# Taps and w1 loaded in halves between pairs of x loads, and logits over interleaved channels

## The chip, the cores and the metric

One core of one Trainium2 chip runs the kernel. The metric is the device time of one execution in microseconds. Before the change, three runs took 309.0, 310.02 and 312.22 us; the median is 310.02 us. A later run is compared with runs of the kernel before on the same chip.

## The reference

All of it is float32. First a causal convolution with weights that differ by position and head, then a soft mixture of experts over all 28672 rows:

```python
w = softmax(weight_gen)                       # [8, 3584, 8 heads, 7 taps], over the taps
x_unf = windows of 7 rows of x                # x: [8, 3584, 192], 8 heads x 24 channels
y = einsum('bshk,bskhg->bshg', w, x_unf)      # -> [28672, 192]
logits = y @ phi                              # phi: [192, 32 slots], 8 experts x 4
d = softmax(logits, axis=0)                   # over the 28672 rows
slot_input = d.T @ y                          # [32, 192]
slot_out[e] = relu(slot_input[e] @ w1[e]) @ w2[e]    # w1: [192, 1024], w2: [1024, 192]
out = softmax(logits, axis=1) @ slot_out      # [28672, 192]
```

## The kernel before

**Blocks and pairs.** The rows are cut into blocks of 26 positions; four of them are a *group* (276 groups), two groups a *pair* (138), four groups a *supergroup* (69, the unit of an x load), four pairs a *block k* (35), eight pairs a *unit u* (17, and a last one of two pairs). So two supergroups make a block k and four a unit.

**Loads.** `loadx(t)` (line 153) is four DMAs, one for each h, of 32 partitions and 96 KB together per DMA; they fill one of five places of `big`, block-diagonally over the four heads of a half. A place is free again when the convolution of the supergroup five earlier has read it. `loadw(c)` (line 158) is one DMA that brings the taps of a *chunk c* into one of three buffers; chunk c serves block k = c. The two parts of the expert weights w1 come as 24 DMAs of 128 partitions and 512 columns (line 571). All are issued on SP in the order of the list `ops`, one after the other; each waits for what it overwrites, and those behind it wait with it.

**The chain of a chunk** (`chain`, line 472): the largest tap (`tap_top`, DVE), the subtraction (`tap_sub`, POOL), the exponential (`tap_exp`, ACT), the sum in three additions (`tap_sum`, POOL), its reciprocal (`tap_inv`, DVE), the product (`tap_mul`, POOL, into `wide`), and a 32x32 transposition (`tap_turn`, DVE) that makes the band matrices (`band`) of one block k.

**TensorE, by block k:** `conv` of the four pairs (16 products of 96 columns each, into a PSUM buffer `cv`; ACT copies it to `tm`), and `xpose`, twelve transpositions whose results ACT copies to `cm`, with channels on partitions. Each odd block also holds, behind its third pair, `dispatch` (line 337), the sum of d.T @ y for the unit before; each even block holds, behind its second pair, `logits` (line 274), 16 products of 208 columns into `ls`. DVE takes the largest logit (`top`, line 285: names mx and mq), TensorE spreads it (`newmax`, line 304), DVE reduces it (`newmax_out`, line 308: nm), ACT takes the exponentials (`dexp`), and DVE transposes them (`dturn`: dt). On even groups the two halves of the heads lie in one order in `cv`, on odd groups in the other, so that three tiles of 128 channels hold a pair; four pieces of phi (`phi_sb`) fit them.

**The order.** Each piece of work is an entry of `ops`: engine, cost, what it reads and writes, and `late`, how much later than the end of its cost its result is there (for a load, the landing). TensorE and SP keep the order of the list. For DVE, ACT and POOL, `model` (line 616) plays the list through with these costs and landings and takes, at each step, the ready entry whose latest allowed time is the earliest. The order found is fixed in the program. An engine does its entries in that order whatever the real times are.

**After the convolution** the last unit is finished, the constants `selO4` (over phi's tile) and `si` are written by POOL (lines 689 and 690), the slot inputs go through the experts (lines 703 to 806), and the output phase (line 832) multiplies, copies and stores 22 MB.

Of the kernel before, what the change touches and what calls it, by code (L numbers as in the profile page):

```python
# [10 lines left out]
ALU = mybir.AluOpType  # L11
# [25 lines left out]
Q = 4  # L37
# [8 lines left out]
def place(t):  # L46
    return t % NXS if t else NXS - 1
# [3 lines left out]
def conv_soft_moe(ctx, tc, xh, wh, phi, w1a, w1b, w2, out):  # L51
# [100 lines left out]
    mq = keep.tile([128, 5], F32, name="mq")  # L152
    def loadx(t):

        for h in range(4):
            SY.dma_start(xbd[32 * h : 32 * h + 32, place(t), h], xh[t, h])

    def loadw(c):
        n = min(CH, NG // 4 - CH * c)
        SY.dma_start(taps[c % NTAP][:, 0:n], wh[c, :, 0:n])  # L160

    ALL = slice(0, CH)
    tops, tsums = {}, {}

# [56 lines left out]
    def conv(p):  # L221
        cv = cvs[p % NCV]
        for par in range(2):
            g = 2 * p + par
            t = g // SGG
            for c in range(2):
                for blk in range(4):
                    o = 4 * GW * (2 * par + (c ^ par))
                    i, b = ((4 * (g % m) + blk) * 2 + c for m in (4, SGG))
                    P.matmul(cv[32 * blk : 32 * blk + T, o : o + 4 * GW],  # L230
                             bands[g // 8 % NBAND][:, g // 4 % CH, :, i],
                             xbd[:, place(t), :, b * GW : (b + 1) * GW], start=True, stop=True)
# [41 lines left out]
    def logits(u, lo=0, hi=UP):  # L274
        hi = min(hi, UNITS[u][1])
        cm = cms[u]
        lp = lss(u).rearrange("p (a b) j -> p a b j", b=2)
        for par in range(2):
            for i in range(2):
                for blk in range(4):  # L280
                    P.matmul(lp[32 * blk : 32 * blk + 32, lo:hi, par, 0:T],  # L281
                             phi_sb[:, 2 * par + i, :], cm[:, lo:hi, 1 if i else 2 * par, blk, :],
                             start=(i == 0), stop=(i == 1))

# [132 lines left out]
    def pace(e, what, src):  # L417
        op(PO, 0.15, [what], [("w2", e), x_of(NSG - NXS + e // 2)], mark, e, src)
        op(SP, 0.4, [("w2", e)], [], loadw2, e)
# [22 lines left out]
    def x_of(t):  # L442
        return ("x", place(t))

    def conv_reads(p):
        return {x_of(g // SGG) for g in (2 * p, 2 * p + 1)} | {("band", p // 4 % NBAND, p // 2 % CH)}

# [6 lines left out]
    op(SP, 0.65, [], [("w", 1, 0), ("w", 1, 1)], loadw, 1, late=2.6)  # L454
    op(SP, 2.6, [], [x_of(0)], loadx, 0, late=2.8)
    op(SP, 0.6, [], [("w", 2, 0), ("w", 2, 1)], loadw, 2, late=3.0)
    op(SP, 1.9, [], [x_of(1)], loadx, 1, late=3.0)
    for t, es in ((2, (PO, AC, AC, AC)), (3, (PO, AC, VE, AC)), (NXS, (PO, PO, AC, AC))):
        for h, e in enumerate(es):
            op(e, 0.77, [], [("z", t, h)], clear, place(t), h, {PO: G, AC: A, VE: V}[e])  # L460
        if t < NXS:
            op(SP, 1.9, [("z", t, h) for h in range(4)], [x_of(t)], loadx, t, late=3.0)
    for i in range(NCV):
# [81 lines left out]
    for k in range(BLOCKS):  # L545
# [8 lines left out]
        for c in range(3, NCH):  # L554
            if k == max(0, c - 2):
                chain(c)
        for c in range(NTAP, NCH):
            if k == max(0, c - 4):
                op(SP, 0.4, [], [("w", c % NTAP, b) for b in range(CH)], loadw, c, late=4.0)
        for t in range(NSG):  # L560
            if (SGG * t + SGG - 1) // (2 * Q) == k:
                if t + NXS < NSG:
                    for i in (NXS - 1, NXS) if t == 0 else (t + NXS,):
                        op(SP, 2.0, [("z", i, h) for h in range(4)], [x_of(i)], loadx, i, late=3.0)
                    if t == 0:
                        op(SP, 0.45, [], ["phi"], SY.dma_start, phi_sb, phi, late=3.0)
                for j in range(2 * (E + E // 2)):
                    if 2 + 5 * j // 2 == t:
                        e, f = j // 2, slice(F // 2 * (j % 2), F // 2 * (j % 2 + 1))
                        to, w, e = (w1a_sb, w1a, e) if e < E else (w1b_sb, w1b, e - E)  # L570
                        op(SP, 0.4, [], [], SY.dma_start, to[:, e, f], w[:, e, f])
        for p in ps:
# [22 lines left out]
    op(TE, 0.19 * n, cm_of(final), [("ls", 1), spare], logits, final)  # L595
    op(VE, 0.4, [], [("ls", 1), "mq"], top, final)
# [91 lines left out]
    bctx = ExitStack()  # L688
    G.tensor_tensor(out=selO4, in0=sel4, in1=selE4, op=ALU.subtract)
    G.memset(si, 0.0)  # L690
    actx.close()
# [12 lines left out]
    P.matmul(pst, accS[:, 1:129], sE, start=True, stop=False)  # L704
    P.matmul(pst[0:96], accS[:, 96:192], sO, start=False, stop=True)
    P.matmul(pst[96:128], accS[:, 0:32], sO, start=False, stop=True)
    V.tensor_copy(siM.rearrange("p (e m) -> p e m", m=DG)[:, :, 0:SE],
# [4 lines left out]
    for r in (0, 64):  # L712
        P.matmul(psu[r : r + 64], accS[:, 129 : D + 1], sE, start=True, stop=False)
        P.matmul(psu[r : r + 64], accS[:, 32:96], sO, start=False, stop=True)
    for u in range(2):
# [168 lines left out]
def _layout(x, weight_gen, moe_phi, moe_w1, moe_w2):  # L884
    import numpy as np

    starts = np.minimum(T * np.arange(NB), S - T)

    xp = np.concatenate([np.zeros((B, KT - 1, D), x.dtype), x], axis=1)
    rows = starts[:, None] + np.arange(L)[None, :]  # L890
    xg = xp[:, rows, :].reshape(NSG, SGG * 4, L, 2, 4, GW)
    xh = xg.transpose(0, 4, 2, 1, 3, 5).reshape(NSG, 4, L, NBC * GW)
# [9 lines left out]
    ph[0] = moe_phi[0:128]
    ph[1, 0:64] = moe_phi[128:192]
    ph[2, 0:32] = moe_phi[160:192]
    ph[2, 32:128] = moe_phi[0:96]
    ph[3, 64:128] = moe_phi[96:160]
    ph = ph.transpose(1, 0, 2)
    w1a = moe_w1[:, 0:128, :].transpose(1, 0, 2)
    w1b = moe_w1[:, 128:D, :].reshape(2, 4, 64, F).transpose(0, 2, 1, 3).reshape(128, 4, F)
    w2 = moe_w2.reshape(E, F // 128, 128, D).transpose(2, 0, 1, 3)  # L910
    return [np.ascontiguousarray(a) for a in (xh, wh, ph, w1a, w1b, w2)]
# [20 lines left out]
```

## Time and profile before

| | before |
|---|---|
| time, median of three runs | 310.02 us (309.0 to 312.22) |
| the profiled execution: time, span | 308.94 us, 307.2 us |
| mean granted TensorE clock | 0.945 |
| busy: PE, DVE, ACT, POOL | 265.4, 197.8, 190.3, 146.5 us |
| SP: issues of x, of taps, of w1 | 276, 35, 24 |
| read from and written to HBM | 46.21 MB, 22.04 MB |

The times of the table are those of one execution; its span runs from the first to the last instruction, and 1.7 us of its time lie around the span. The views used below are: the chain of waits (the work that ended last, in order of time: start, length, what), the windows (busy time of each engine in a stretch, the granted clock and the DMA share), the groups of instructions (by line, engine and operation, with the mean of one), the waits, and the timeline. On SP, a row of the timeline joins neighbouring issues of one kind, and its length runs from the first issue to the end of the last.

### The profile page before, as it was taken

To read this page: it belongs to the slowest core of one execution; us is meant where nothing else is said; L and a number is where in the kernel's file an instruction comes from. 1 tells how busy PE (TensorE), PEld (TensorE's weight loads), DVE (VectorE), ACT (ScalarE), POOL (GpSimd) and SP (SyncE) were. 2 spreads that over 40 slices of the span, in tenths; PEclk is the share of its full clock that TensorE was granted. 3 is DMA by queue.
4 is the path that set the end of the run, shared out by engine and by line. 5 is a ranking of instruction groups with operands and counts; after the bars stand their busy time and mean duration, and the time that the engine had idled before them with its cause. 6 is when DMAs were issued, how large, how long until landed. Compare 5 with 4: busy or idle time off the path is not lost.

```text
span 307.2 us, 15262 instructions
## 1 busy us (share of the span) xinstructions
PE 265.4 (86%) x6646; PEld 213.6 (70%) x6646; DVE 197.8 (64%) x337; ACT 190.3 (62%) x399; POOL 146.5 (48%) x254
## 2 busy tenths in 40 slices
PE   8898996999998999899899989999999888899100
PEld 8887975889887988789788878898768622233000
DVE  8867738775975957868478568573158489994100
ACT  9886673767685778667566666675422188786300
POOL 8856456654568194774654553520027345540000
PEclk9999998999999999999999999999999999879555
DMA  6758666867675767767567667657647079999994
GB/s 184 217 171 236 201 199 195 208 178 207 197 211 150 225 188 207 207 192 212 168 183 212 189 185 211 189 156 227 217 121 296 2 303 403 399 398 398 399 399 177
DMA packets 30161, 69.24 MB, mean 225 GB/s; under 512 B 6288, under 2 KB 11152, under 8 KB 30096
## 3 DMA queue, kind: packets, MB, share of 16 engines
q1 hardware_dynamic: 30096, 68.28, 69.2%
q8 instruction: 52, 0.85, 1.1%
q14 instruction: 13, 0.11, 0.1%
HBM read 46.21 MB, written 22.04 MB: 222 GB/s over the span
## 4 chain that ended last, share of the span: by engine, by line
PE 73%; DVE 6%; DMA 6%; issue 5%; ACT 2%; POOL 2%; DVEq 0%; POOLq 0%; ACTq 0%
PE cv L230 31%; PE pt L250 15%; PE ls L281 8%; PE acb L346 8%; PE po L818 5%; DMA out<-big 4%; PE so L763 2%; PE hpb L742 2%; PE acb L306 2%; DMA taps<-wh 2%; DVE big L825 1%; ACT big L825 1%; DVE band L206 1%; DVE big L362 1%; DVE cT L404 1%
## 5 line engine op out<-in xcount | busy, mean ns | idle before, releaser
L230 PE MATMUL cv<-big,band 128*26 128x96 f32 x4416 | 112.0, 250 | 4.0 <-issue 2.6
L230 PEld LDWEIGHTS cv<-big,band 128*26 128x26 f32 x4416 | 100.8, 130 | 13.8 <-issue 8.1
L236 ACT COPY tm<-cv 128x384 f32<-128x384 f32 x138 | 66.5, 484 | 62.8 <-PE cv L230 62.5
L206 DVE STREAM_TRANSPOSE band<-wide 128x1664 f32<-128x1664 f32 (+1 forms) x37 | 65.4, 1771 | 6.1 <-POOL wide L202 6.0
L250 PE MATMUL pt<-ident,tm 122*128 122x122 f32 x414 | 51.0, 273 | 0.0
L257 ACT COPY cm<-pt 128x416 f32<-128x416 f32 x103 | 48.1, 512 | 1.7 <-PE pt L250 0.6
L250 PEld LDWEIGHTS pt<-ident,tm 122*128 122x128 f32 x414 | 44.7, 145 | 2.3
L202 POOL TENSOR_TENSOR wide<-exps,sum 128x364 f32<-128x364 f32 (+1 forms) x36 | 28.4, 791 | 24.9 <-DVE sum L194 18.6
L818 PE MATMUL po<-cT,so 32*128 32x442 f32 (+3 forms) x256 | 35.4, 644 | 5.6 <-DVE big L825 3.0
L175 POOL TENSOR_TENSOR taps<-taps,top 128x364 f32<-128x364 f32 (+1 forms) x36 | 28.5, 793 | 18.3 <-DVE top L171 17.9
L825 ACT COPY big<-po 128x884 f32<-128x884 f32 (+2 forms) x33 | 28.5, 894 | 9.3 <-PE po L818 5.3
L188 POOL TENSOR_TENSOR si<-exps 128x208 f32<-128x208 f32 x32 | 20.2, 632 | 28.4 <-ACT exps L179 28.0
L818 PEld LDWEIGHTS po<-cT,so 32*128 32x128 f32 (+1 forms) x256 | 12.3, 172 | 27.5 <-ACT big L825 15.7
L281 PE MATMUL ls<-cm,phi_sb 128*32 128x208 f32 x544 | 29.1, 338 | 2.0 <-issue 1.9
L346 PE MATMUL acb<-tm,dt 128*32 128x193 f32 x544 | 27.4, 328 | 3.3 <-issue 3.3
L288 DVE TENSOR_REDUCE mx<-ls 128x1 f32<-128x416 f32 x17 | 10.0, 588 | 28.1 <-PE ls L281 28.1
L87 POOL TENSOR_TENSOR LT<-LT,rm 128x544 f32<-128x544 f32 (+1 forms) x16 | 17.9, 1119 | 17.0 <-DVE rm L85 17.0
L171 DVE TENSOR_REDUCE top<-taps 128x52 f32<-128x364 f32 (+1 forms) x37 | 17.7, 484 | 12.8 <-DMA taps<-wh 12.0
L281 PEld LDWEIGHTS ls<-cm,phi_sb 128*32 128x32 f32 x544 | 17.8, 109 | 7.9 <-issue 3.6
L346 PEld LDWEIGHTS acb<-tm,dt 128*32 128x32 f32 x544 | 17.8, 110 | 7.4 <-issue 4.7
L99 POOL TENSOR_TENSOR LT<-LT,sm 128x544 f32<-128x544 f32 (+1 forms) x16 | 17.9, 1120 | 6.3 <-DVE sm L97 6.2
L825 DVE COPY big<-po 128x884 f32<-128x884 f32 (+2 forms) x16 | 16.7, 1047 | 6.2 <-ACT big L825 2.2
(113 smaller groups left out, 262.3 us busy)
## 6 DMA issues: line engine op xcount, KB each, us to landing
big<-xh SPq DMA_DIRECT2D x276, 96.0 KB, 3.2
out<-big SPq DMA_DIRECT2D x36, 442.0 KB, 6.9
taps<-wh SPq DMA_DIRECT2D x34, 182.0 KB, 3.7
big<-w SPq DMA_DIRECT2D x8, 768.0 KB, 4.5
out<-big SPq DMA_DIRECT2D x11, 468.0 KB, 4.7
w1a_sb<-w1a SPq DMA_DIRECT2D x16, 256.0 KB, 4.2
w1b_sb<-w1b SPq DMA_DIRECT2D x8, 256.0 KB, 3.6
out<-big SPq DMA_DIRECT2D x2, 234.0 KB, 2.3
```

The costliest lines, as they stand in the source:

```text
L175: eng.tensor_tensor(out=t, in0=t, in1=each(tops.pop((c, b.start)), b.stop - b.start), op=ALU.subtract)
L188: eng.tensor_tensor(out=s, in0=t[:, :, :, 0:4], in1=t[:, :, :, 4:8], op=ALU.add)
L202: eng.tensor_tensor(out=dst, in0=exps[c % NEX][:, b, :, 0:KT], in1=each(m, n), op=ALU.mult)
L206: V.transpose(bands[c % NBAND][:, b].rearrange("p b j l -> p (b j l)"), wide[:, b].rearrange("p b j -> p (b j)"))
L230: P.matmul(cv[32 * blk : 32 * blk + T, o : o + 4 * GW], bands[g // 8 % NBAND][:, g // 4 % CH, :, i], xbd[:, place(t), :, b * GW : (b + 1) ...
L236: copy(tms[u % NTM][:, pr, 1 : 2 * D + 1], cvs[p % NCV][:, 0 : 2 * D])
L250: P.transpose(pt[:, at, 0:TR], tms[u % NTM][0:TR, pr, 1 + 128 * i : 129 + 128 * i], ident[0:TR, 0:TR])
L257: copy(cms[u].rearrange("p a i b j -> p (a i b) j")[:, at : at + n], pts.pop((k, j)).rearrange("p i (b j) -> p (i b) j", j=32)[:, 0:n, 0:T])
L281: P.matmul(lp[32 * blk : 32 * blk + 32, lo:hi, par, 0:T], phi_sb[:, 2 * par + i, :], cm[:, lo:hi, 1 if i else 2 * par, blk, :], start=(i = ...
L346: P.matmul(ac[32 * q : 32 * q + 32], dt[:, g, :], tm[:, g // 2, o : o + D + 1], start=(g < 4), stop=(g + 4 >= 2 * n))
L818: P.matmul(po[dst : dst + hi - lo, at, 0 : n * T], so[32 * q : 32 * q + 32, lo:hi], cT[32 * q : 32 * q + 32, g0 : g0 + n, 0:T], start=True ...
L825: (V.tensor_copy if done[1] % 3 == 1 else A.copy)(ot.rearrange("p (q c) -> p q c", c=n * T), po[:, 0 : len(qs), 0 : n * T])
```

## The change

1. **Halves between pairs.** `loadx` issues two of its four DMAs at a time; `loadw` can load 64 of the 128 partitions; w1 comes in 48 DMAs of 64 partitions. In the list, the two halves of a chunk of taps stand each behind the first pair of x DMAs of a supergroup, where the whole chunk stood ahead of the two supergroups. From the fourth chunk on, taps are two DMAs where they were one.
2. **Landings in the list.** `late` of x goes from 3.0 to 3.8 and the cost of four x DMAs from 2.0 to 2.3; `late` of the taps goes from 4.0 to 5.2.
3. **One product of 416 columns.** The products of `conv` now write the 96 columns of a half of the heads interleaved, at a step of eight columns, so that the first 64 or 128 channels of a group are the same channels in every tile; on odd groups the host turns the channels of x by eight. The first and the third tile of a pair then take the same piece of phi, and one product of 416 columns over both replaces two of 208. The host orders the rows of phi and w1 alike.
4. **Constants earlier.** `selO4` and the zeroing of `si` become entries of the list; in the product that uses `selO4`, two products (96 and 32 rows) become one.

```diff
-    def loadx(t):
-        for h in range(4):
+    def loadx(t, hs=range(4)):
+        for h in hs:
             SY.dma_start(xbd[32 * h : 32 * h + 32, place(t), h], xh[t, h])
-    def loadw(c):
+    def loadw(c, r=slice(0, 128)):
         n = min(CH, NG // 4 - CH * c)
-        SY.dma_start(taps[c % NTAP][:, 0:n], wh[c, :, 0:n])
+        SY.dma_start(taps[c % NTAP][r, 0:n], wh[c, r, 0:n])
+    def loadw1(j):
+        e, f, r = j // 4, slice(F // 2 * (j // 2 % 2), F // 2 * (j // 2 % 2 + 1)), HALF[j % 2]
+        to, w, e = (w1a_sb, w1a, e) if e < E else (w1b_sb, w1b, e - E)
+        SY.dma_start(to[r, e, f], w[r, e, f])
...
             for c in range(2):
+                to = cv[:, D * par : D * par + D].rearrange("p (g e) -> p e g", e=H)[:, 4 * c : 4 * c + 4]
                 for blk in range(4):
-                    o = 4 * GW * (2 * par + (c ^ par))
-                    P.matmul(cv[32 * blk : 32 * blk + T, o : o + 4 * GW],
+                    P.matmul(to[32 * blk : 32 * blk + T],
...
+        for blk in range(4):
+            P.matmul(lp[32 * blk : 32 * blk + 32, lo:hi, :, 0:T], phi_sb[:, 0, :],
+                     cm[:, lo:hi, 0:3:2, blk, :], start=True, stop=False)
         for par in range(2):
-            for i in range(2):
-                for blk in range(4):
-                    P.matmul(lp[32 * blk : 32 * blk + 32, lo:hi, par, 0:T],
-                             phi_sb[:, 2 * par + i, :], cm[:, lo:hi, 1 if i else 2 * par, blk, :],
-                             start=(i == 0), stop=(i == 1))
+            for blk in range(4):
+                P.matmul(lp[32 * blk : 32 * blk + 32, lo:hi, par, 0:T], phi_sb[:, 1 + par, :],
+                         cm[:, lo:hi, 1, blk, :], start=False, stop=(par == 1))
...
-        for c in range(NTAP, NCH):
-            if k == max(0, c - 4):
-                op(SP, 0.4, [], [("w", c % NTAP, b) for b in range(CH)], loadw, c, late=4.0)
-        for t in range(NSG):
...
-                        op(SP, 2.0, [("z", i, h) for h in range(4)], [x_of(i)], loadx, i, late=3.0)
...
+        cs = [c for c in range(NTAP, NCH) if k == max(0, c - 4)]
+        parts = [(c, i) for c in cs for i in range(2)]
+        for t in (2 * k, 2 * k + 1):
+            for i in (NXS - 1, NXS) if t == 0 else (t + NXS,) if t + NXS < NSG else ():
+                for j in range(2):
+                    op(SP, 1.15, [("z", i, h) for h in (2 * j, 2 * j + 1)], [x_of(i)[j]],
+                       loadx, i, (2 * j, 2 * j + 1), late=3.8)
+                    if j == 0 and parts and t:
+                        c, h = parts.pop(0)
+                        op(SP, 0.4, [], [("w", c % NTAP, h)], loadw, c, HALF[h], late=5.2)
...
+                for j in range(48):
+                    if 2 + 5 * j // 4 == t:
+                        op(SP, 0.42, [], [], loadw1, j)
+        for c, h in parts:
+            op(SP, 0.4, [], [("w", c % NTAP, h)], loadw, c, HALF[h], late=5.2)
...
+    op(PO, 0.45, ["fold"], ["si"], lambda: G.memset(si, 0.0))
+    op(TE, 0.19 * n, cm_of(final), [("ls", 1), spare, "phi"], logits, final)
+    op(PO, 0.5, ["sel4"], ["phi"], lambda: G.tensor_tensor(out=selO4, in0=sel4, in1=selE4, op=ALU.subtract))
...
-    G.tensor_tensor(out=selO4, in0=sel4, in1=selE4, op=ALU.subtract)
-    G.memset(si, 0.0)
...
-    P.matmul(pst[0:96], accS[:, 96:192], sO, start=False, stop=True)
-    P.matmul(pst[96:128], accS[:, 0:32], sO, start=False, stop=True)
+    P.matmul(pst, accS[:, 64:D], sO, start=False, stop=True)
```

Three places show how instructions move. The first is SP at the start of the program, behind the x of the first supergroup; taps_84, taps_85 and taps_86 are the three buffers of taps, and the first taps row is chunk 2. Before:

```order
L160 DMA taps_86<-wh 128x364
L156 DMA big<-xh 32x768 x12
L160 DMA taps_84<-wh 128x364
L160 DMA taps_85<-wh 128x364
L156 DMA big<-xh 32x768 x8
L686 DMA phi_sb<-phi 128x128
```

After:

```order
L160 DMA taps_86<-wh 128x364
L156 DMA big<-xh 32x768 x20
L698 DMA phi_sb<-phi 128x128
L156 DMA big<-xh 32x768 x2
L160 DMA taps_84<-wh 64x364
L156 DMA big<-xh 32x768 x2
L160 DMA taps_84<-wh 64x364
L160 DMA taps_85<-wh 64x364 x2
L156 DMA big<-xh 32x768 x2
L160 DMA taps_86<-wh 64x364
L156 DMA big<-xh 32x768 x2
L165 DMA w1a_sb<-w1a 64x512
```

Chunks 3 and 4 stood behind 12 x DMAs and now stand behind 22 and 24 of them and phi.

The second place is DVE around the first unit's logits. In the names, the number behind top and sum is the chunk, the number behind mx, nm and dt the unit, and band2 and band0 are the buffers of chunks 2 and 3. Before:

```order
L171 TENSOR_REDUCE top3_0_387<-taps0_84 128x52
L171 TENSOR_REDUCE top4_0_390<-taps1_85 128x52
L206 STREAM_TRANSPOSE band2_92<-wide_89 128x1664
L194 RECIPROCAL sum3_0_453<-sum3_0_453 128x52
L288 TENSOR_REDUCE mx0_525<-ls_99 128x1
L290 TENSOR_SCALAR mq_131<-ls_99,mx0_525 128x4
L206 STREAM_TRANSPOSE band0_90<-wide_89 128x1664
L310 TENSOR_REDUCE nm0_577<-acb_100 128x1
```

After:

```order
L212 STREAM_TRANSPOSE band2_92<-wide_89 128x1664
L295 TENSOR_REDUCE mx0_506<-ls_99 128x1
L297 TENSOR_SCALAR mq_131<-ls_99,mx0_506 128x4
L317 TENSOR_REDUCE nm0_538<-acb_100 128x1
L177 TENSOR_REDUCE top3_0_554<-taps0_84 128x52
L334 STREAM_TRANSPOSE dt0_559<-dd_95 128x512
L177 TENSOR_REDUCE top4_0_563<-taps1_85 128x52
L301 STREAM_TRANSPOSE LT_65<-ls_99 128x512
L200 RECIPROCAL sum3_0_570<-sum3_0_570 128x52
L212 STREAM_TRANSPOSE band0_90<-wide_89 128x1664
```

The first step of chunk 3 stood ahead of chunk 2's band and now stands behind the reduction nm0. On TensorE the order of the blocks is the same in both.

The third place is DVE around the logits of unit 2, with the same names (band1 is the buffer of chunk 7). Before:

```order
L354 SCALAR_TENSOR_TENSOR accS_66<-accS_66,al1_949,acb_100 128x193
L194 RECIPROCAL sum7_0_951<-sum7_0_951 128x52
L171 TENSOR_REDUCE top9_0_998<-taps0_84 128x52
L206 STREAM_TRANSPOSE band1_91<-wide_89 128x1664
L288 TENSOR_REDUCE mx2_1064<-ls_99 128x1
```

After:

```order
L361 SCALAR_TENSOR_TENSOR accS_66<-accS_66,al1_919,acb_100 128x193
L177 TENSOR_REDUCE top8_0_992<-taps2_86 128x52
L200 RECIPROCAL sum7_0_957<-sum7_0_957 128x52
L212 STREAM_TRANSPOSE band1_91<-wide_89 128x1664
L295 TENSOR_REDUCE mx2_1077<-ls_99 128x1
```

The chunk whose taps DVE waits for ahead of mx2 is the eighth where it was the ninth.

More of the change, by code (lines that the diff above doesn't have):

```diff
@@ L417, in pace @@
     def pace(e, what, src):
-        op(PO, 0.15, [what], [("w2", e), x_of(NSG - NXS + e // 2)], mark, e, src)
+        op(PO, 0.15, [what], [("w2", e), *x_of(NSG - NXS + e // 2)], mark, e, src)
         op(SP, 0.4, [("w2", e)], [], loadw2, e)
@@ L442, in x_of @@
     def x_of(t):
-        return ("x", place(t))
+        return [("x", place(t), i) for i in range(2)]
     def conv_reads(p):
-        return {x_of(g // SGG) for g in (2 * p, 2 * p + 1)} | {("band", p // 4 % NBAND, p // 2 % CH)}
+        return {x for g in (2 * p, 2 * p + 1) for x in x_of(g // SGG)} | {("band", p // 4 % NBAND, p // 2 % CH)}
     def tm_of(p):
@@ L461, in conv_soft_moe @@
         if t < NXS:
-            op(SP, 1.9, [("z", t, h) for h in range(4)], [x_of(t)], loadx, t, late=3.0)
+            op(SP, 1.9, [("z", t, h) for h in range(4)], x_of(t), loadx, t, late=3.0)
     for i in range(NCV):
@@ L556, in conv_soft_moe @@
                 chain(c)
-        for c in range(NTAP, NCH):
-            if k == max(0, c - 4):
-                op(SP, 0.4, [], [("w", c % NTAP, b) for b in range(CH)], loadw, c, late=4.0)
-        for t in range(NSG):
-            if (SGG * t + SGG - 1) // (2 * Q) == k:
-                if t + NXS < NSG:
-                    for i in (NXS - 1, NXS) if t == 0 else (t + NXS,):
-                        op(SP, 2.0, [("z", i, h) for h in range(4)], [x_of(i)], loadx, i, late=3.0)
[L565 to L571, printed above, removed]
+        cs = [c for c in range(NTAP, NCH) if k == max(0, c - 4)]
[8 more added lines that the diff above has]
+                        op(SP, 0.4, [], [("w", c % NTAP, h)], loadw, c, HALF[h], late=5.2)
+            if t == 0:
+                op(SP, 0.45, [], ["phi"], SY.dma_start, phi_sb, phi, late=3.0)
+            if 2 <= t < NSG:
+                for j in range(48):
[3 more added lines that the diff above has]
+            op(SP, 0.4, [], [("w", c % NTAP, h)], loadw, c, HALF[h], late=5.2)
         for p in ps:
@@ L713, in conv_soft_moe @@
         P.matmul(psu[r : r + 64], accS[:, 129 : D + 1], sE, start=True, stop=False)
-        P.matmul(psu[r : r + 64], accS[:, 32:96], sO, start=False, stop=True)
+        P.matmul(psu[r : r + 64], accS[:, 0:64], sO, start=False, stop=True)
     for u in range(2):
@@ L899, in _layout @@
     wh = wt.transpose(0, 5, 2, 4, 1, 3, 6).reshape(NCH, 128, CH, T, KT)
+    chan = np.arange(D).reshape(H, GW).T.reshape(D)
+    lo, hi = chan[0:128], chan[128:D]
     ph = np.zeros((4, 128, NS), moe_phi.dtype)
[L902 to L906, printed above, removed]
+    ph[0] = moe_phi[lo]
+    ph[1, 0:64] = moe_phi[hi]
+    ph[2, 64:128] = moe_phi[hi]
     ph = ph.transpose(1, 0, 2)
-    w1a = moe_w1[:, 0:128, :].transpose(1, 0, 2)
-    w1b = moe_w1[:, 128:D, :].reshape(2, 4, 64, F).transpose(0, 2, 1, 3).reshape(128, 4, F)
+    w1a = moe_w1[:, lo, :].transpose(1, 0, 2)
+    w1b = moe_w1[:, hi, :].reshape(2, 4, 64, F).transpose(0, 2, 1, 3).reshape(128, 4, F)
     w2 = moe_w2.reshape(E, F // 128, 128, D).transpose(2, 0, 1, 3)
```

8 lines of the change are left out of this document (5 added, 3 removed).

## The prediction

> **What bounds the kernel now.** I read the windows first: length, then busy time and count of PE, PEld, DVE, ACT and POOL, the granted clock, the DMA share and GB/s.
>
> ```profile
> 24.07:201.07 177.00, 167.14 (x4849) 147.30 (x4852) 123.86 (x197) 117.56 (x266) 101.55 (x177) 0.99 0.68 197
> 102.67:114.38 11.71, 11.71 (x351) 10.33 (x354) 8.32 (x17) 8.61 (x21) 7.18 (x11) 1.00 0.71 204
> 46.00:56.00 10.00, 7.23 (x191) 6.63 (x190) 8.22 (x13) 4.03 (x10) 5.40 (x11) 0.83 0.72 196
> ```
>
> The first stretch is most of the convolution, the second one unit of it in which PE is never idle (351 matmuls; the first has 4849, which is fourteen units of 346). A unit costs 177.00 / 14 = 12.64 us, and 11.71 where nothing waits: 13.1 us are lost. TensorE is the bound and DMA (0.68) is not. The third stretch holds the largest loss: PE idle, and 10.00 x (1 - 0.83) = 1.7 us of clock.
>
> ```profile
> span 307.2 us, 15262 instructions
> DMA  6758666867675767767567667657647079999994
> ```
>
> A slice is 7.68 us. From the 34th slice on, 253.4 us, the DMA engines are full with stores, and before it stand the experts, which need the whole convolution. So a microsecond gained or lost on TensorE before that moves the end by a microsecond.
>
> Next the chain of waits about the third stretch, and the row of PE's waits (total, times, longest):
>
> ```profile
> 42.38 4.68 DMA taps<-wh
> ...
> 47.61 1.82 DVE band L206
> 49.43 0.49 DVE mx L288
> ...
> 50.31 0.36 PE acb L306 x2
> ```
>
> ```profile
> PE acb L306 <- DVE mq L290: 3.2, 2, 2.8
> ```
>
> The taps of chunk 9 are issued at 42.38 and take 4.68 us; DVE stands before them, and behind on DVE stand a band and mx of unit 2, for whose spread PE waits 2.8 us. With the clock, 4.5 us of the 13.1 are here. The other 8.6 are small and spread.
>
> **The change part by part.**
>
> *The wait at mx2.* In the third piece of the order, DVE stands ahead of mx2 before the first step of chunk 8, no longer chunk 9; chunk 8's loads are a block older. The wait goes, and its clock: -4.5. What is late next is the band of chunk 7, which stood there before too.
>
> *Chunk 3's chain.* It now begins behind nm0, and its end is what PE's block 3 needs. PE's rows at that place:
>
> ```profile
> 22.45 0.32 PE acb L306 x2
> 22.77 1.31 PE pt L250 x12
> 24.07 2.14 PE cv L230 x96
> ```
>
> Block 3 starts at 24.07 with no wait. In the changed order DVE can do nm0 from 22.8 and top3 after it, then the chain runs through four engines; the groups (count, busy, mean ns of one, idle before):
>
> ```profile
> L171 DVE TENSOR_REDUCE top<-taps 128x52 f32<-128x364 f32 (+1 forms) x37 | 17.7, 484 | 12.8 <-DMA taps<-wh 12.0 <-POOL taps L175 0.7
> L175 POOL TENSOR_TENSOR taps<-taps,top 128x364 f32<-128x364 f32 (+1 forms) x36 | 28.5, 793 | 18.3 <-DVE top L171 17.9
> L318 ACT ACTIVATE dd<-ls,nm 128x416 f32<-128x416 f32 x17 | 10.5, 616 | 2.4 <-DVE nm L310 1.6
> L257 ACT COPY cm<-pt 128x416 f32<-128x416 f32 x103 | 48.1, 512 | 1.7 <-PE pt L250 0.6
> L179 ACT ACTIVATE exps<-taps 128x364 f32<-128x364 f32 (+1 forms) x37 | 17.9, 493 | 3.9 <-POOL taps L175 3.9
> L188 POOL TENSOR_TENSOR si<-exps 128x208 f32<-128x208 f32 x32 | 20.2, 632 | 28.4 <-ACT exps L179 28.0
> L189 POOL TENSOR_TENSOR si<-si 128x104 f32<-128x104 f32 x32 | 11.6, 362 | 2.5
> L190 POOL TENSOR_TENSOR sum<-si 128x52 f32<-128x52 f32 x32 | 9.2, 288 | 2.5
> L194 DVE RECIPROCAL sum<-sum 128x52 f32<-128x52 f32 (+1 forms) x37 | 16.3, 441 | 2.6 <-POOL sum L190 2.4
> L202 POOL TENSOR_TENSOR wide<-exps,sum 128x364 f32<-128x364 f32 (+1 forms) x36 | 28.4, 791 | 24.9 <-DVE sum L194 18.6 <-ACT tm L236 5.0 <-DMA big<-xh 1.2
> L206 DVE STREAM_TRANSPOSE band<-wide 128x1664 f32<-128x1664 f32 (+1 forms) x37 | 65.4, 1771 | 6.1 <-POOL wide L202 6.0
> ```
>
> Newmax ends at 22.77; I put the end of nm0, a small reduction, at 22.9. From there: top 0.48, subtraction 0.79, exponential 0.49, sum 0.63 + 0.36 + 0.29, reciprocal 0.44, product 0.79, turn 1.77 make 6.04 us, so the band is there at 28.9 and PE waits 4.9 us: the lower bound, with every engine free. ACT is not free: in its new order, the exponentials of unit 0 (0.62, from 23.0) and three copies (0.51 each) stand ahead of chunk 3's exponential, which stood ahead of them. That begins at 25.1 instead of 24.2: +0.9. On POOL, chunk 4's subtraction (0.79) may come in ahead of the product, and handing over between engines adds some tenths. I take 6.3 us and keep 4.9 and 7.5 (both intrusions whole, plus that subtraction before the sums too). Nothing covers this: PE's next work, dispatch and conv, is behind block 3 in its own list.
>
> A wait of 2.8 us cost 1.7 us of clock in the third stretch; this one is longer. I take the same 1.7, bounds 0 and twice it, 3.4. The clock was 1.00 at the wait for nothing, and I have no row of a second wait in this phase.
>
> *Issues on SP.* Rows of SP's timeline (start, length from the first issue to the end of the last) and of the DMA issues (count, size, time from issue to landing):
>
> ```profile
> 16.88 1.78 SPq L156 DMA_DIRECT2D big<-xh  x4
> ...
> 30.80 0.35 SPq L160 DMA_DIRECT2D taps<-wh  x1
> ...
> 36.84 4.97 SPq L156 DMA_DIRECT2D big<-xh  x8
> ...
> 42.38 0.38 SPq L160 DMA_DIRECT2D taps<-wh  x1
> ```
>
> ```profile
> big<-xh SPq DMA_DIRECT2D x276, 96.0 KB, 3.2
> taps<-wh SPq DMA_DIRECT2D x34, 182.0 KB, 3.7
> w1a_sb<-w1a SPq DMA_DIRECT2D x16, 256.0 KB, 4.2
> ```
>
> An issue of x costs 1.78 / 4 = 0.445 us on SP, and one of 182 KB 0.35 to 0.38: half the bytes do not halve it. From 30.80 to 42.38 SP issues a unit's 20 (16 of x, two of taps, two of w1) in 11.58 us, 0.579 each, with whatever waits are among them. After, a unit has 16 of x, four halves of taps and 0.8 x 4 = 3.2 halves of w1: 23.2. At 0.445 that is 10.3 us and SP is free; at 0.579 it is 13.4. I take 0.55, nearer the stretch, since the eight x at 36.84 alone took 0.62 each: 12.76 us a unit. PE without the wait at mx2 needs 12.64 - 4.5 / 14 = 12.32. The excess is 0.44 x 13.5 units (after block 3, while w1 is loading) = 5.9 us, less the lead that x has on TensorE. A place that is free has four supergroups ahead of it, 11.71 us, less 3.2 to land and 1.78 to issue, so 6.7 at most; I take half, 3.4. **SP costs 2.5 us**; bounds 0 (0.445) and 15.0 (0.579, no lead: 1.11 x 13.5). The 55 more issues (31 of taps, 24 of w1) also queue x behind a taps half that waits for its buffer; three buffers are as before, so I charge nothing for that beyond this range.
>
> The half loads land sooner or later than 3.7 and 4.2 us: no row tells. The Trainium skill ("DMA: Bandwidth & Descriptors", section "Rules for kernel authors") says of two transfers to disjoint partition halves "Don't bother — they serialize", and to use one of 128 partitions. By that, halves bring nothing and the sum would keep the SP term alone; the x row agrees in kind, since 96 KB take 3.2 us where 256 KB take 4.2.
>
> *Writes of conv at a step of eight columns.* No row has it. The nearest are the same products as they stand, and the logits (TensorE's chain, records of four column groups):
>
> ```profile
> 28.67 0.66 PE cv L230 x32
> ...
> 32.21 1.41 PE ls L281 x32
> ```
>
> ```profile
> L230 PE MATMUL cv<-big,band 128*26 128x96 f32 x4416 | 112.0, 250 | 4.0 <-issue 2.6
> ```
>
> Thirty-two products are eight rounds of four; 0.66 / 8 / 96 = 0.86 ns per column with runs of 96 outputs, 1.41 / 8 / 208 = 0.85 with the logits' runs of 26. Shorter runs cost nothing, so I take 0 for a step of eight, bounds 0 and a doubling of the row, +112 us.
>
> *One product of 416 columns.* The columns per group stay 832 a unit, and the two rates show no fixed cost of a product: 0. A quarter of the products goes, so the gain is at most a quarter of 1.41, 0.35 us a unit, 6.0 over 17.
>
> *Larger landings in the list.* They act only through the order, counted above.
>
> *The constants.* PE waits for them once:
>
> ```profile
> 229.32 0.45 POOL L689 TENSOR_TENSOR phi_sb<-sel,selE 128x128 f32<-128x128 f32 x1
> ...
> 229.83 0.35 PE L705 MATMUL pst<-phi_sb,accS 128*96 128x32 f32 x2 [0.24 <-POOL phi_sb L689]
> 230.11 0.25 PE L706 MATMUL pst<-phi_sb,accS 128*32 128x32 f32 x2
> ```
>
> The wait of 0.24 and part of the second product go: -0.4 (bounds -0.5 and 0).
>
> The profiled execution took 308.94 us: 308.94 - 4.5 + 6.3 + 1.7 + 2.5 - 0.4 = 314.5. It lies 1.1 below the median of the runs shown, 310.02, so the forecast is **315.6 us**.
>
> **The rivals.**
>
> *A. SP keeps pace and the small losses go too.* The remaining 8.6 us of waits have no owner: L230 lost 2.6 to "issue". If they come of late x, the smaller loads between pairs of x and the later landings in the list may end them: 13.5 x (12.64 - 11.71) = 12.6, of which 4.5 is counted already, so -8.1 in the place of +2.5. Then 308.94 - 4.5 + 6.3 + 1.7 - 0.4 - 8.1 = 303.9, with 1.1 **305.0**. It decides where an issue costs no more than 11.71 / 23.2 = 0.505 us. For it: 0.445 when x stands alone. Against: the 0.62 of 36.84.
>
> *B. SP becomes the bound.* At 0.579 an issue, 13.43 us a unit against 12.32, 15.0 over 13.5 units, less 3.4: +11.6 for the 2.5, **324.7**. For it, the whole stretch of 30.80; against, that this includes waits for places. It decides above 12.32 / 23.2 = 0.531 us.
>
> *C. The interleaved writes are slow.* Each of 4416 products writes every eighth column. If that doubled the row of 112.0, it would be hidden by nothing: 315.6 - 2.5 (SP is no bound then) + 112 = **425**, and already a tenth of it would be 11 us. Against: equal rates of 0.85 and 0.86. The Trainium skill ("PSUM — Partial Sum Buffer", section "Specifications (TRN2)") gives lines of 8 bytes and says that any non-contiguous access slows matmuls significantly; the short runs of the logits do not bear that out, but a run of one is not among the rows.
>
> *D. It evens out.* The wait at block 3 is at its lower end, the clock does not fall and SP has time: 308.94 - 4.5 + 4.9 - 0.4 = 308.9, **310.0**. For it: each is an end that a row gives; against: three of them at once.
>
> **How the numbers follow.** Forecast 0.47, with an own range of 311 to 321 (block 3 from 4.9, clock from 0 or to 3.4, SP 0 to 5.9); A 0.13, B 0.13, C 0.06, D 0.21. From 307 to 326 only A and C are out, 0.19. This measurement tells about 1% from no change, so the limits are 306.9 and 313.1: faster is A, 0.13; within is D and a fifth of the forecast's case, 0.30; slower is the rest, 0.57.
>
> **What would show it.** Right: a wait of PE of about 6 us for the band ahead of block 3, at 24 to 30 us, a granted clock below 1 behind it, and none for mq in unit 2; SP without a pause from 30 us on, at about 0.55 us an issue, and PE's weight loads waiting for x by a few tenths a unit. Rival A shows as units of 11.7 us, B as units of 13.4 with waits for x, C as a mean of L230's products well over 250 ns, D as block 3 at 29 us with a full clock behind. The forecast is wrong if block 3 starts before 28 us: then top3 did not wait for nm0, or the chain overlapped what I put in a row.

## The result, and the profile after

The changed kernel takes 347.98 us (median of four runs, 346.67 to 348.83) beside 311.12 us for the kernel before on the same chip. The ratio is 1.121, with a 95% interval from 1.112 to 1.129: some 37 us slower. Ratios are taken over the faster of two states in which the executions of one kernel fall, and medians over all runs, so the two can differ; the profiles of the last two experiments below are of the slower state. The forecast of 315.6 us had the side right and the size wrong by a factor of six to seven (+36.9 us for +5.6), and the time lies outside the range of 311 to 321 us.

The profiled execution of the changed kernel took 348.83 us, its span is 347.1 us. First its windows, with the columns as in the prediction: the 6 us ahead of block 3, and most of the convolution.

```profile
24.00:30.00 6.00, 0.14 (x4) 0.14 (x8) 3.74 (x5) 1.33 (x4) 4.07 (x9) 0.76 0.58 163
24.00:220.00 196.00, 161.29 (x4458) 138.93 (x4458) 117.50 (x185) 109.87 (x250) 95.52 (x165) 0.95 0.57 163
```

TensorE is busy for 161.29 of 196 us, where it was busy for 167.14 of 177. The DMA share fell from 0.68 to 0.57: the DMA engines are not what is full. TensorE's waits (total, times, longest):

```profile
PE cv L236 <- DVE band L212: 11.3, 5, 6.2
PE acb L313 <- DVE mq L297: 9.5, 5, 4.5
PE acb L313 <- POOL si L195: 5.4, 2, 3.3
PE acb L313 <- POOL sum L196: 5.1, 2, 4.1
PE cv L236 <- DMA big<-xh: 4.2, 4, 1.7
PE acb L313 <- POOL taps L181: 3.1, 3, 1.8
```

Only one of these is the wait ahead of block 3 (6.2). All others but the one for x (`big`) name DVE and POOL, but those wait themselves. The groups, with the idle time before them behind the last bar:

```profile
L236 PE MATMUL cv<-big,band 128*26 128x96 f32 x4416 | 115.7, 259 | 17.7 <-DVE band L212 11.3 <-DMA big<-xh 4.2 <-issue 1.5
L181 POOL TENSOR_TENSOR taps<-taps,top 128x364 f32<-128x364 f32 (+1 forms) x36 | 28.4, 789 | 55.0 <-DVE top L177 47.5 <-DMA big<-xh 4.0 <-DVE nm L317 3.4
L177 DVE TENSOR_REDUCE top<-taps 128x52 f32<-128x364 f32 (+1 forms) x37 | 18.2, 497 | 59.2 <-DMA taps<-wh 48.5 <-DMA big<-xh 9.7 <-POOL taps L181 0.7
L285 PE MATMUL ls<-cm,phi_sb 128*32 128x416 f32 x136 | 15.0, 513 | 0.5 <-ACT cm L263 0.5
L289 PE MATMUL ls<-cm,phi_sb 128*32 128x208 f32 x272 | 15.1, 338 | 0.0
```

The first step of the chunks, top, stood 48.5 us idle for the taps, where it stood 12.0 before, and all else of the chunk, with whatever stands behind it on DVE and POOL, comes as late. The loads do not land later once issued (count, size, issue to landing):

```profile
big<-xh SPq DMA_DIRECT2D x276, 96.0 KB, 2.9
taps<-wh SPq DMA_DIRECT2D x62, 91.0 KB, 2.5
w1a_sb<-w1a SPq DMA_DIRECT2D x32, 128.0 KB, 3.3
```

All three are quicker than before (3.2, 3.7 and 4.2). They are issued late. A piece of SP's timeline (start, length from the first issue to the end of the last):

```profile
78.71 0.47 SPq L160 DMA_DIRECT2D taps<-wh  x1
79.22 1.04 SPq L156 DMA_DIRECT2D big<-xh  x2
80.31 0.47 SPq L165 DMA_DIRECT2D w1a_sb<-w1a  x1
80.88 0.99 SPq L156 DMA_DIRECT2D big<-xh  x2
...
86.59 1.04 SPq L156 DMA_DIRECT2D big<-xh  x2
87.68 1.62 SPq L165 DMA_DIRECT2D w1a_sb<-w1a  x1
```

SP issues without a pause: the next row begins 0.04 to 0.10 us behind the end of the last. From SP's rows between the 65th and the 209th x issue, nine units, I worked out for the two kernels and the ten experiments how long a unit is, how many issues it has, and the distance from the start of one issue to the start of the next: its mean, its mean where it is under 0.75 us ("plain"), and the number of longer ones. The last two columns tell a price from a wait: the *pauses*, which are gaps of over 0.15 us between the end of an issue and the start of the next, per unit, and the mean distance without them.

```
                         unit us  issues  mean us  plain us  longer: count, mean us  pauses us  mean without
before                   12.35    19.6    0.632    0.464     39  1.22                1.30       0.565
after                    14.72    23.1    0.637    0.536     27  1.31                0.08       0.633
e1_whole                 12.19    19.6    0.623    0.462     33  1.32                1.08       0.568
e2_w1_whole              13.56    21.6    0.629    0.510     28  1.34                0.09       0.625
e4_w1_act                13.14    20.0    0.657    0.527     25  1.46                0.08       0.653
e5_interleaved           12.10    19.6    0.619    0.464     30  1.37                0.48       0.594
e6_landings              14.97    23.1    0.648    0.536     28  1.37                0.08       0.644
e7_tiny                  13.37    23.6    0.568    0.467     26  1.29                0.20       0.559
e10_early_whole          12.17    19.6    0.622    0.464     29  1.42                0.27       0.609
e11_columns              13.56    23.1    0.587    0.471     27  1.36                0.09       0.583
e8_before_w1_act         12.44    18.0    0.691    0.464     37  1.46                2.32       0.562
e12_early_whole_act      12.50    18.0    0.695    0.468     39  1.41                2.35       0.564
```

Issues times mean distance is the length of the unit in every row, whatever holds the kernel, since the mean contains the pauses. It is a price only where the pauses are near nothing.

A unit of the changed kernel is 14.72 us long on SP, with next to no pause. That is 2.37 us more than before, where SP stands 1.30 us of a unit; over the 14.75 units in which w1 loads (supergroups 2 to 60) it makes 35 us. TensorE's side agrees: from the start of block 3 to its last product the convolution takes 232.3 us (29.86 to 262.2) for 198.3 (24.07 to 222.4). These 34.0 us and the 5.8 by which block 3 starts later are the difference between the two spans, 347.1 and 307.2 us. And in the chain of waits from 60 to 270 us, SP's issues of x have 10.3% and the flights of the taps 10.6%; before, neither is among its larger parts.

### The profile page after: what moved, and what is told of

It reads as the page before. It is cut to its first block, busy times and chain, and to the rows that moved or that the text cites. A ratio compares the mean times of both kernels' runs of the same rounds, so it can differ in the third digit from the quotient of the medians.

```text
span 347.1 us, 15063 instructions
## 1 busy us (share of the span) xinstructions
PE 272.5 (79%) x6500; PEld 216.2 (62%) x6500; DVE 198.7 (57%) x337; ACT 189.6 (55%) x399; POOL 146.9 (42%) x254
## 4 chain that ended last, share of the span: by engine, by line
PE 38%; DMA 16%; DVE 12%; POOL 9%; issue 8%; SPq 8%; ACT 4%; POOLq 0%; DVEq 0%; ACTq 0%
PE cv L236 16%; PE pt L256 8%; DMA taps<-wh 6%; SPq L156 6%; DVE band L212 5%; DMA big<-xh 4%; DMA out<-big 4%; PE acb L353 3%; POOL taps L181 3%; PE po L827 2%; PE so L772 2%; PE hpb L751 2%; POOL si L194 1%; DVE top L177 1%; PE ls L289 1%
## 5 line engine op out<-in xcount | busy, mean ns | idle before, releaser
L236 PE MATMUL cv<-big,band 128*26 128x96 f32 x4416 | 115.7, 259 | 17.7 <-DVE band L212 11.3
L236 PEld LDWEIGHTS cv<-big,band 128*26 128x26 f32 x4416 | 105.4, 133 | 28.4 <-DVE band L212 13.2
L242 ACT COPY tm<-cv 128x384 f32<-128x384 f32 x138 | 65.8, 482 | 61.7 <-PE cv L236 60.8
L256 PE MATMUL pt<-ident,tm 122*128 122x122 f32 x414 | 55.8, 287 | 2.9 <-ACT tm L242 2.9
L177 DVE TENSOR_REDUCE top<-taps 128x52 f32<-128x364 f32 (+1 forms) x37 | 18.2, 497 | 59.2 <-DMA taps<-wh 48.5
L256 PEld LDWEIGHTS pt<-ident,tm 122*128 122x128 f32 x414 | 48.1, 153 | 6.2 <-ACT tm L242 3.8
L185 ACT ACTIVATE exps<-taps 128x364 f32<-128x364 f32 (+1 forms) x37 | 18.2, 491 | 35.4 <-POOL taps L181 29.2
L353 PE MATMUL acb<-tm,dt 128*32 128x193 f32 x544 | 25.7, 328 | 0.0
L313 PE MATMUL acb<-mq,sel 128*128 128x5 f32 (+1 forms) x34 | 6.6, 264 | 23.1 <-DVE mq L297 9.5
L200 DVE RECIPROCAL sum<-sum 128x52 f32<-128x52 f32 (+1 forms) x37 | 16.4, 443 | 9.3 <-POOL sum L196 9.0
L313 PEld LDWEIGHTS acb<-mq,sel 128*128 128x128 f32 x34 | 5.5, 202 | 25.7 <-issue 14.2
```

The lines of the kernel that those rows point to most:

```text
L177: V.tensor_reduce(out=m, in_=taps[c % NTAP][:, b], axis=AX.X, op=ALU.max)
L236: P.matmul(to[32 * blk : 32 * blk + T], bands[g // 8 % NBAND][:, g // 4 % CH, :, i], xbd[:, place(t), :, b * GW : (b + 1) * GW], start=Tru ...
L242: copy(tms[u % NTM][:, pr, 1 : 2 * D + 1], cvs[p % NCV][:, 0 : 2 * D])
L256: P.transpose(pt[:, at, 0:TR], tms[u % NTM][0:TR, pr, 1 + 128 * i : 129 + 128 * i], ident[0:TR, 0:TR])
L353: P.matmul(ac[32 * q : 32 * q + 32], dt[:, g, :], tm[:, g // 2, o : o + D + 1], start=(g < 4), stop=(g + 4 >= 2 * n))
```

## The experiments

**Theory S**: SP sets the pace, by what its issues take. **Theory O**: the new order on the engines makes the waits. **Theory P**: the interleaved products are slower. The first four runs are one group on one chip, beside 309.41 us for the kernel before; the changed kernel was run in another group, so differences from it are taken between ratios, in shares of about 310 us.

**Whole loads in the same order.** The second halves are left out of SP's work and the first ones made whole; the list, from which the order is found, is the same.

```diff
-        SY.dma_start(taps[c % NTAP][r, 0:n], wh[c, r, 0:n])
+        r.start or SY.dma_start(taps[c % NTAP][:, 0:n], wh[c, :, 0:n])
-        SY.dma_start(to[r, e, f], w[r, e, f])
+        j % 2 or SY.dma_start(to[:, e, f], w[:, e, f])
```

> The list, and with it the order on PE, DVE, ACT and POOL, stays that of the changed kernel; only, where the first half of a chunk or of a w1 piece stood, the whole is loaded in one DMA, and the second half's place is empty. SP then issues some 19.6 DMAs a unit where the changed kernel issues 23.2. Theory S (the changed kernel is held by the number of issues on SP, about 0.64 us each, 23 a unit = 14.7 us): at 19.6 a unit SP needs 12.2 us and PE's own 11.7 to 12.3 count again; the wait ahead of block 3 (6 us) stays: 308 to 320 us. Theory O (the order on the engines, with the late first steps of the chunks, makes the loss): it is the same order, so over 335 us. Theory P (the interleaved products are slower): unchanged, about 347 us.

Measured: 310.79 us, ratio 1.015 (1.007 to 1.023). That is within what S gave. With the order unchanged, O falls but for one place, and with the products unchanged P falls too. That place is the wait ahead of block 3, still whole in this kernel's waits:

```profile
PE cv L236 <- DVE band L212: 7.2, 2, 6.2
```

**Only w1 whole.** The second of the two edits alone.

> As the changed kernel, but w1 in 24 whole loads at the places of the first halves; the taps stay in halves. About 1.6 issues a unit fewer (21.6). Theory S: 24 issues of 0.64 us fewer on the path, 13 to 16 us: 331 to 336 us. Theory O or P: no change, 345 to 350 us. If only the halves of the taps matter (their place or their landing): no change either.

Measured: 329.26 us, ratio 1.075 (1.068 to 1.083). Between this and the changed kernel lie 24 issues and 4.5%, 14 us, and from here to whole taps 31 issues and 6.0%, 18.6 us: some 0.6 us an issue in both. The 14 us are in the 13 to 16 expected; the time itself lies below the 331 to 336. Both halves of the loss are of the same kind.

**The halves of w1 issued by ScalarE.**

```diff
-        SY.dma_start(to[r, e, f], w[r, e, f])
+        A.dma_start(to[r, e, f], w[r, e, f])
```

> As the changed kernel, with the same 48 half loads of w1, issued by ScalarE instead of SyncE. The bytes, the number and the sizes of the transfers are the same; SP has 20 issues a unit. Theory S: 48 issues of 0.64 us leave SP, 31 us, as far as PE's own pace allows: 316 to 324 us. If the transfers themselves (the DMA engines, their packets) are what is full or slow: no change, 343 to 350 us.

Measured: 323.14 us, ratio 1.053 (1.042 to 1.065), as S had it. The same transfers with the same bytes cost 6.7%, some 21 us, less when another engine issues them: it is SP's time, not the transfers. The kernel before is not reached. SP still does not pause (0.08 us a unit): its unit of 13.14 us, with the halves of the taps left in it, holds this version too. ScalarE may pay a part, since TensorE now waits for its copies; how much is not shown:

```profile
PE ls L285 <- ACT cm L263: 7.2, 7, 1.6
```

The Trainium skill ("DMA: Bandwidth & Descriptors", section "Rules for kernel authors") says of spreading DMAs over engines that it only saves the sequencer's issue time; here just that was worth some 21 us.

**The landings of before in the list.**

```diff
-                    op(SP, 1.15, [...], [x_of(i)[j]], loadx, i, (2 * j, 2 * j + 1), late=3.8)
+                    op(SP, 1.0, [...], [x_of(i)[j]], loadx, i, (2 * j, 2 * j + 1), late=3.0)
-                        op(SP, 0.4, [], [("w", c % NTAP, h)], loadw, c, HALF[h], late=5.2)
+                        op(SP, 0.4, [], [("w", c % NTAP, h)], loadw, c, HALF[h], late=4.0)
```

> As the changed kernel, but with the landings and costs of before in the list (x 3.0 instead of 3.8 and 2.0 for four instead of 2.3, taps 4.0 instead of 5.2). On DVE the first step of chunk 3 then stands ahead of nm0. Theory S: the wait ahead of block 3 gets shorter, but from there SP's pace holds the kernel as before, so most of the gain is given back: 342 to 348 us. Theory O (the waits come from the order that the larger landings give, and add up): the 6 us ahead of block 3 and some of the later ones go, under 340 us.

Measured: 350.55 us, ratio 1.146 (1.135 to 1.157), 2.5% above the changed kernel and above both expectations. Neither had the wait ahead of block 3 right: it became longer, not shorter. On DVE (start, length, group, and in brackets the idle time before it) top3 is ahead of nm now, but so is the first step of chunk 5 ahead of the band of chunk 3, and its taps are still on the way:

```profile
22.19 0.53 DVE L177 TENSOR_REDUCE top<-taps 128x52 f32<-128x364 f32 x1 [0.55 <-DMA taps<-wh]
22.63 0.15 DVE L317 TENSOR_REDUCE nm<-acb 128x1 f32<-128x4 f32 x1
...
29.75 0.53 DVE L177 TENSOR_REDUCE top<-taps 128x52 f32<-128x364 f32 x1 [2.78 <-DMA taps<-wh]
30.20 0.47 DVE L200 RECIPROCAL sum<-sum 128x52 f32<-128x52 f32 x1
30.59 1.85 DVE L212 STREAM_TRANSPOSE band<-wide 128x1664 f32<-128x1664 f32 x1
```

Block 3 began at 32.50 instead of 29.86. The larger landings do not make the loss.

The next four are one group on another chip, beside 307.21 us for the kernel before.

**The interleaved products and the constants alone.** The changed kernel, with the part of the list that loads as before (each chunk whole ahead of the x, w1 whole, x in fours, the landings of before).

```diff
+        for c in range(NTAP, NCH):
+            if k == max(0, c - 4):
+                op(SP, 0.4, [], [("w", c % NTAP, b) for b in range(CH)], loadw, c, late=4.0)
...
-                for j in range(2):
-                    op(SP, 1.15, [...], [x_of(i)[j]], loadx, i, (2 * j, 2 * j + 1), late=3.8)
+                op(SP, 2.0, [...], x_of(i), loadx, i, late=3.0)
```

> The third and fourth parts of the change alone: interleaved products of conv, one product of 416 columns, the constants earlier; taps and w1 whole, at the places and with the landings that they have in the list of before. Theory S: these parts cost nothing, 307 to 311 us, with L230's products (a line or two lower here) at a mean of 250 to 260 ns. Theory P (writes at a step of eight are slower, hidden in the changed kernel behind SP): over 314 us. That the constants bring their 0.4 us can't be told by this measurement.

Measured: 305.82 us, ratio 0.996 (0.992 to 1.000). That is below the 307 to 311 expected, and no slower than the kernel before. Its row for conv:

```profile
L237 PE MATMUL cv<-big,band 128*26 128x96 f32 x4416 | 110.4, 250 | 5.9 <-issue 3.8
```

250 ns, as before. Writing at a step of eight columns costs nothing that shows.

**More issues without bytes.** The kernel before, with a 0.5 KB DMA in each supergroup.

```diff
         for h in range(4):
             SY.dma_start(xbd[32 * h : 32 * h + 32, place(t), h], xh[t, h])
+            if h == 1 and 10 <= t:
+                SY.dma_start(spot[:, 8 * (t % 4) : 8 * (t % 4) + 8], phi[0:16, 0, 0:8])
```

> The kernel before, with one more DMA of 0.5 KB into a tile that nothing reads, between the second and the third x DMA of each supergroup from the eleventh on: 59 issues more, 23.6 a unit, and 0.03 MB in all. Theory S by number alone: about as many issues as the changed kernel, so 330 to 348 us, by the price of such an issue (0.46 to 0.64 us on SP). If bytes, half loads or the order on the engines make the loss: 309 to 313 us.

Measured: 329.82 us, ratio 1.075 (1.064 to 1.086). 59 issues that carry 0.03 MB in all cost some 23 us. This is the number alone: no half, no new order, no bytes. It lies just below the 330 to 348 that S gave, as such an issue is no dearer than a whole load (plain 0.467 us), and SP's pauses are down from 1.30 to 0.20 us a unit. In its timeline a tiny issue takes as long as one of 256 KB:

```profile
86.80 0.42 SPq L159 DMA_DIRECT2D spot<-phi  x1
87.27 0.88 SPq L157 DMA_DIRECT2D big<-xh  x2
88.19 0.42 SPq L689 DMA_DIRECT2D w1a_sb<-w1a  x1
```

**Halves by columns.** The same number of halves at the same places, each of 128 partitions and half of the columns.

```diff
-        SY.dma_start(taps[c % NTAP][r, 0:n], wh[c, r, 0:n])
+        b = slice(0, n) if r.stop - r.start == 128 or n < CH else slice(r.start // 64, r.start // 64 + 1)
+        (n < CH and r.start) or SY.dma_start(taps[c % NTAP][:, b], wh[c, :, b])
-        SY.dma_start(to[r, e, f], w[r, e, f])
+        f = slice(f.start + F // 4 * (j % 2), f.start + F // 4 * (j % 2 + 1))
+        SY.dma_start(to[:, e, f], w[:, e, f])
```

> As the changed kernel, but each half is all 128 partitions with half of the columns (taps 128 x 182, w1 128 x 256), not 64 partitions with all of them. The number of issues, their places and the bytes are the same. If a 64-partition issue and the x issue behind it are dearer on SP (0.47 and 0.58 us, where a whole load takes 0.38 and the x behind it 0.37): plain issues come down from 0.54 to 0.46 us, 23.2 x 0.07 = 1.7 us a unit, 20 to 25 us in all: 322 to 330 us. If the number alone counts: no change, 344 to 350 us.

Measured: 323.63 us, ratio 1.056 (1.048 to 1.063). Taps, w1 and x behind them in its timeline:

```profile
93.78 0.42 SPq L161 DMA_DIRECT2D taps<-wh  x1
94.24 0.89 SPq L156 DMA_DIRECT2D big<-xh  x2
...
99.28 0.43 SPq L167 DMA_DIRECT2D w1a_sb<-w1a  x1
```

The half of 64 partitions takes 0.47 us, this one 0.42; two x behind it 0.89 against 0.99 to 1.04. The plain distance comes down from 0.536 to 0.471 us, over the 20 plain ones of a unit 1.3 us, and the unit from 14.72 to 13.56. The time is in the 322 to 330 us expected.

**Whole loads, and chunks 3 and 4 early again.**

```diff
-        cs = [c for c in range(NTAP, NCH) if k == max(0, c - 4)]
+        cs = [c for c in range(NTAP, NCH) if 0 < k == c - 4]
+        for c in range(NTAP, 5) if k == 0 else ():
+            op(SP, 0.4, [], [("w", c % NTAP, 0), ("w", c % NTAP, 1)], loadw, c, late=4.0)
```

> As the run with whole loads at the places of the first halves, but with the taps of chunks 3 and 4 where they stood before, ahead of the x of the fifth place; on DVE the first steps of chunks 3 and 4 then stand ahead of chunk 2's band again. Theory S with the prediction's price of the wait ahead of block 3: that wait (6.2 us in the run with whole loads) and its clock go, and SP has room: 301 to 305 us, faster than before. Rival: what the wait ahead of block 3 held back, SP holds back instead, or the wait at mx2 is back: 308 to 312 us.

Measured: 304.75 us, ratio 0.994 (0.990 to 0.998), with the second edit besides those of the run with whole loads. The profiled execution took 303.85 us; its block 3 stands in the chain at

```profile
22.74 1.31 PE pt L256 x12
24.05 2.14 PE cv L236 x96
```

so the wait is gone, and with it 2.1% (1.015 against 0.994), 6.5 us; by the two intervals that may be 4 to 9. This version is ahead of the kernel before by 0.6%, which is hardly clear of nothing, and isn't told apart from the interleaved products alone (0.996). The time is at the upper end of the 301 to 305 us expected.

The last two were run in another group, beside 309.65 us for the kernel before.

**The kernel before with w1 issued by ScalarE.**

```diff
-                        op(SP, 0.4, [], [], SY.dma_start, to[:, e, f], w[:, e, f])
+                        op(SP, 0.4, [], [], A.dma_start, to[:, e, f], w[:, e, f])
```

> The kernel before, with its 24 whole loads of w1 issued by ScalarE instead of SyncE; the order on DVE and TensorE is the same. If SP holds the kernel before too (19.6 issues a unit at 0.62 us are 12.2 us, TensorE alone needs 11.7): 24 issues off SP are up to 15 us, of which TensorE's pace leaves some 6: 300 to 304 us. If SP has room in the kernel before: 306 to 309 us, or a little slower by ScalarE's part.

Measured: 310.0 us, ratio 0.997 (0.991 to 1.002). 24 issues fewer brought nothing. The idea that SP held the kernel before as well falls: with fewer issues SP only pauses longer, 2.32 us a unit for 1.30. At 19.6 issues a unit their price is hidden in such pauses; at 23 there are none left.

**Both: whole, early, and w1 by ScalarE.**

> As the run with whole loads and the early chunks 3 and 4, with w1 issued by ScalarE instead of SyncE: 18 issues a unit on SP, about 11 us. If SP still holds that kernel in places: 298 to 302 us. If TensorE and the chains hold it: 303 to 306 us.

Measured: six runs from 306.5 to 313.58 us, beside 305.12 to 314.06 for the kernel before. No run came near the 298 to 302 us of an SP that still holds it, and SP pauses 2.35 us a unit, where it paused 0.27 without the move. So SP seems to have no part there that could be taken away; whether the move makes the version a little slower stays open.

## Why the prediction was wrong

**Where the loss is from.** By the ratios of the experiments, in shares of about 310 us and each to some 3 us: the 64-partition shape of the halves 1.121 - 1.056, 6.5%, 20 us; the number of issues 1.056 - 1.015, 4.1%, 13 us; the late chunks 3 and 4 1.015 - 0.994, 2.1%, 6.5 us; and the rest of the change -0.6%, -2 us. These hold for taking the parts away in this order. They do not simply add up: the number alone, put on the kernel before, cost 7.5%, 23 us.

**The step that failed: the price of an issue.** The count was right (23.2 forecast, 23.1 found). The price was taken as 0.55 us, between 0.445 and 0.579, and was 0.633 without pauses (0.637 with them): above my upper end. The larger part of the miss is the shape. I took the price of a half from rows of whole loads, and said that half the bytes do not halve it; that it could be dearer I did not weigh, though the description of the change names the 64 partitions. Halves by columns, the same number, cost 0.583, and whole loads in the kernel before 0.565, so for whole loads my 0.55 was nearly right.

The second part is how little room such a price leaves. The SP term was the small difference of 12.76 and 12.32 us, 0.44 a unit; at 23.1 issues, 0.03 us on the price adds 0.7. Even at 0.583 a unit is 13.5 us and the excess over 13.5 units 15 us. With the measured 14.72 it is 2.40 a unit, and 32.4 us in place of 5.9.

**The lead.** I took 3.4 us off for x's lead on TensorE. The 34.0 us that TensorE loses from block 3 on, beside SP's 35, leave room for about 1 us. The first place of the loss was not x but the taps, which gate a block through a chain of 6 us, and which SP's order puts behind x. Whether the lead was used up ahead of block 3 is not shown.

**The wait ahead of block 3** was right in its path and its size: it was forecast as 6.3 us, and it is this row of the changed kernel's TensorE:

```profile
29.86 1.50 PE L236 MATMUL cv<-big,band 128*26 128x96 f32 x31 [6.22 <-DVE band L212]
```

Part of that agreement is luck. Chunk 3's exponential began at 24.28, near the 24.2 of a free ACT and not at the 25.1 that I put, and block 3 at 29.86 and not at 24.07 + 6.3 = 30.37; but TensorE stood ready at 23.64, 0.4 us earlier than before.

The clock of 0.76 in the first window above costs nothing by itself, since TensorE is idle there. What it costs is in block 3's first 96 products, at a granted clock of 0.50 from 29.86 to 33.93. In the chain of waits:

```profile
29.86 4.07 PE cv L236 x96
```

They took 2.14 us before: 1.9 us, where 1.7 was put. Restoring the early loads gave 6.5 us of the forecast 8.0.

**The wait at mx2** did not go. DVE does stand before chunk 8's first step there, and no longer before chunk 9's. But the second half of chunk 8 is issued only at 49.53 us and lands at 53.29, where before all of chunk 8 was issued at 36.37 and chunk 9 at 42.38; DVE stands 5.95 us before that step, and unit 2 waits longer than before (4.07 us for 2.8):

```profile
58.02 0.56 PE L313 MATMUL acb<-mq,sel 128*128 128x5 f32 x2 [4.07 <-POOL sum L196]
```

This is a second term that failed: -4.5 assumed that loads a block older have landed. With SP behind, age in the list is not age in time. With whole loads and the early chunks, TensorE's waits for mq in all are 0.4 us, so the step holds where SP has room.

**The terms set to nothing** held. conv's products are 250 ns in the run of the interleaved products alone, and 259 in the changed kernel, whose clock is lower (0.918 against 0.945 over the span). The logits are 15.0 + 15.1 us where they were 29.1: one product of 416 columns is no gain. On the interleaved writes the Trainium skill's rule ("PSUM — Partial Sum Buffer", section "Specifications (TRN2)"), that non-contiguous access slows matmuls significantly, does not hold for this product of 96 columns; the measurement decides.

**The rivals.** B was the mechanism, at 0.13 and with the time of 324.7, 23 us too low by the same price and the same 3.4 us of lead. Its deciding point for 23.2 issues, 0.531 us, is passed by every mean without pauses in the table, that of whole loads too; the kernel before is not held because at 19.6 issues its 0.565 makes 11.1 us. A, C and D did not occur. The Trainium skill's rule on halves ("DMA: Bandwidth & Descriptors", section "Rules for kernel authors") agrees with the runs in that halves brought no time, and the halves by partitions were the worse of the two kinds; that they serialize no run shows. A half does land sooner (2.5 us for 3.7, 3.3 for 4.2).

## What to carry to other kernels

Count a queue's issues per unit of work, and price them from stretches in which the queue does not pause, and from rows of the very shape that is to be issued. The mean distance over a stretch with pauses is no price: times the count it gives back the length of the stretch. When the count times the price comes near the pace of the bounding engine, a small error in it decides, and a transfer cut in two is paid in full once the pauses are used up. The rows of DVE and POOL that end TensorE's waits are then only messengers: look for the first wait behind them, and for a queue whose issues follow each other without a pause. An earlier place in a list helps a load only as long as its queue keeps up.

## What the runs showed of the hardware that I had not expected

**Number, not bytes.** A DMA of 0.5 KB, one of 91 KB over 128 partitions and one of 256 KB all keep SP for about 0.42 us (whole taps, 182 KB, for 0.37).

**Halves of 64 partitions are dearer than whole loads or halves by columns, for the one behind as well.** The mean plain distance from an issue to the next in the nine units, by the issue's kind and the kind of the one ahead of it, for the kernel before, the changed one and the run with halves by columns:

```
                              before          halves, 64 partitions    halves by columns
taps behind x                 0.49            0.52                     0.45
x behind taps                 0.41            0.62                     0.47
w1 behind x                   0.54            0.57                     0.52
x behind w1                   0.39            0.57                     0.42
x behind x                    0.47            0.48                     0.48
```

The larger part falls on the x issue behind a half of 64 partitions, 0.15 to 0.2 us. Why is not shown; the x issues themselves are the same. It is not the number of partitions alone, since an x issue, of 32, costs 0.47 to 0.48 behind another in all three.

**One issue in seven to nine is itself 0.8 to 1.1 us longer**, in all twelve kernels: 18 to 26 issues in the nine units take over 0.7 us, 1.2 to 1.5 on average, where the others take 0.40 to 0.48. (The column "longer" above has pauses in it as well.) In the changed kernel that is 0.10 us of each issue, a sixth of the mean distance. In the traces of the changed kernel and of the version with whole loads and early chunks, 32 and 40 transfers of the instruction queue lie between 20 and 200 us, and by each lies one such issue; in that of the kernel before, by 36 of 39. No run changed their number, so it stays open whether they are the cause.
